# ScalarE copies two kinds of small results out of their PSUM banks, and VectorE works on the copies

## The chip, the core and the metric

The kernel runs on one core of one Trainium2 chip. The metric is device time in microseconds (us), the median of several runs of the whole program. The engines are named as in the profile: PE is TensorE (matrix products), DVE is VectorE, ACT is ScalarE, POOL is GpSimd, SP is the engine whose queue issues nearly all DMAs. A "bank" is a PSUM bank, into which PE writes its results and from which DVE and ACT read them.

## The reference

Two blocks follow one another. The first is attention in which a query sees only the keys that were assigned to the same cluster (4 batches, 8 heads, 768 positions, head width 64, 16 clusters per head). The second is a feed-forward net over the 3072 positions (512 wide, 2048 hidden) with a squared ReLU.

```python
q_assign = argmax(einsum('bhsd,hcd->bhsc', q_n, c_n))   # q, k, centroids normalised
k_assign = argmax(einsum('bhsd,hcd->bhsc', k_n, c_n))
scores = where(q_assign[:, :, :, None] == k_assign[:, :, None, :], q @ k.T / sqrt(D), -1e9)
attn = exp(scores - max);  attn = attn / (sum(attn) + 1e-9)
x = (attn @ v) with heads side by side                  # (3072, 512)
out = (maximum(x @ w_in, 0) ** 2) @ w_out
```

## The kernel before, in words

**Units.** Heads are taken in pairs, so a batch has four pairs (HP = 4) and there are 16 in all. The 768 queries of a pair are taken in two halves h of 384 (TB = 384), and the 768 keys in chunks of 128 (c), two chunks to a unit. Batch 0 goes first through the first halves of all four pairs, then through their second halves; from batch 1 on, a pair's two halves follow each other. Below, (1, 1) means pair 1, second half. All of the change lies in the second halves of batch 0, with one part of it in the preparation for pair 4, the first pair of batch 1.

**A unit's work.** `scores` (L447) has PE form the scores of two chunks in two score banks (records "sc"), ACT takes their exponential (L474), and in batch 0 the mask is already inside the product, so the result is the tile `ex`. From batch 1 on DVE multiplies by the mask (L478). `times_v` (L505) multiplies by v into a bank "av". In all but batch 0's first halves POOL adds the `ex` tiles up over the chunks (L488, L490) into `acc`.

**The end of a half.** `add_up` (L531) has PE multiply `acc` by ones into a bank "sm" of 128x192, and DVE takes the reciprocal, `r` (L545). Two DMAs carry `r` to DRAM (L548) and to a table for a later test (L552), two more bring it back spread over 64 partitions each as `rb` (L551). `finish` (L561) multiplies av by rb into xT (L564, DVE). The tile `r` has one buffer, `rb` has two.

**Preparation of a pair.** For pair 4 and later, the words of q and k are split by ACT (L282), written to DRAM (L283) and read back turned (L293). `logits` (L301) multiplies by the centroids into a bank "lg", and ACT copies it (L312). `number` (L318) turns the logits with three PE transposes into a bank "lt" (L322); DVE takes the maximum over the clusters (L345), compares (L346), weights by an order (L349), takes the maximum again (L352) and casts (L364). `spread` (L401) sends the cluster numbers through DRAM to all partitions.

**Fill work.** Between the attention's products PE is given products of the feed-forward net of batch 0 (`ffn`, L573): "ph" (L578), evacuated by ACT (L585, L586) into gT, and later "po" (L591). While batch 0 runs, the weights are also rounded, 32 pieces in all, each with two ACT instructions (L150, L152), three DVE instructions (L155, L159, L163) and one POOL instruction (L167); their loads (L139) may run four pieces ahead.

**The banks.** These banks come from one ring of two:

```python
ps_f = ctx.enter_context(tc.tile_pool(name="ps_f", bufs=2, space=PSUM))
def bank(name, shape):
    return ps_f.tile(shape, F32, name=name, tag="f")
```

Every "ph", "po", "lg", "lt", "pt", "pb" and, in the halves that the change touches, "sm" takes the next bank of this ring, and has to wait until the tile two places earlier has been read. The scheduler orders each engine's instructions ahead of time; each engine then works its own stream in that order.

## Time and profile before

| | |
|---|---|
| median of 7 runs | 977.77 us (975.77 to 978.62) |
| the profiled execution | 978.39 us, of it 976.6 us span |
| PE busy | 957.2 us, 98% of the span |
| DVE, POOL, ACT busy | 564.4, 380.7, 315.6 us |

The stretches around the change, busy us of each engine:

| stretch (us) | length | PE | DVE | ACT | POOL | granted clock |
|---|---|---|---|---|---|---|
| 80 to 100 | 20 | 18.14 | 19.50 | 15.42 | 17.44 | 1.00 |
| 100 to 120 | 20 | 19.84 | 12.32 | 12.37 | 15.25 | 0.91 |
| 120 to 140 | 20 | 18.13 | 14.71 | 11.33 | 12.22 | 1.00 |
| 140 to 165 | 25 | 23.53 | 16.13 | 12.93 | 15.33 | 1.00 |
| 165 to 190 | 25 | 24.86 | 15.95 | 12.22 | 14.47 | 1.00 |

Read it so: a product of 384 columns has two records, so the "ph" of one f, four products, has eight. A line of the timeline gives start, length, engine, line, operation, operands, number of instructions, and in brackets how long the engine stood idle before them and what ended that. Line numbers in the text and the profile lines are those of the kernel before.

### The profile page before, as it was taken

The page shows a single profiled execution, that of the slowest core. Times are in us where ns is not written, and L with a number is a line of the kernel's source. Part 1 is how long each engine was busy: PE and PEld are TensorE (multiplying, and loading weights), DVE is VectorE, ACT ScalarE, POOL GpSimd, SP SyncE. Part 2 cuts the span into 40 slices and gives each one's busy share as a digit, 9 for nine tenths or more (in the row PEclk, how much of TensorE's full clock was granted, in tenths as well). Part 3 has the DMA queues.
Part 4 walks back from the last instruction along what each step waited for, and adds up shares of the span by engine and source line. Part 5 has one row for each costly group of instructions (what it writes and reads, how often), then busy time and mean ns, then how long its engine had stood idle before and what let it go on. Part 6 is the DMA issues. An engine that isn't in the chain of part 4 may idle for free.

```text
span 976.6 us, 12064 instructions
## 1 busy us (share of the span) xinstructions
PE 957.2 (98%) x4479; PEld 551.6 (56%) x4479; DVE 564.4 (58%) x913; ACT 315.6 (32%) x511; POOL 380.7 (39%) x277
## 2 busy tenths in 40 slices
PE   8999999999999999999999999999999999999997
PEld 4544444443444444444443556888556888556886
DVE  5779666666566665666657966531556431656331
ACT  5887645443444555544322111000111000111000
POOL 1338756555656556565567331002231002331000
PEclk9999999999999999999999999999999999999999
DMA  9667672444545354452310000000000000000000
GB/s 245 197 204 210 182 191 68 118 109 116 133 108 147 105 130 116 108 134 74 77 44 9 19 1 0 22 22 22 1 0 1 22 22 21 1 1 0 22 22 25
DMA packets 127746, 74.54 MB, mean 76 GB/s; under 512 B 90944, under 2 KB 119104, under 8 KB 127680
## 3 DMA queue, kind: packets, MB, share of 16 engines
q1 hardware_dynamic: 125968, 73.26, 28.3%
q8 instruction: 38, 0.62, 0.3%
q10 hardware_dynamic: 1712, 0.43, 0.2%
q14 instruction: 28, 0.23, 0.1%
HBM read 48.27 MB, written 15.86 MB: 66 GB/s over the span
## 4 chain that ended last, share of the span: by engine, by line
PE 89%; DVE 3%; ACT 3%; DMA 2%; issue 1%; SPq 1%; POOL 0%; ACTq 0%; DVEq 0%; POOLq 0%
PE bank L701 22%; PE bank L670 22%; PE po L591 8%; PE ph L578 7%; PE sc L91 7%; PE sc L94 6%; PE av L91 6%; PE av L94 5%; PE sm L91 1%; ACT ex L474 1%; PE lg L91 1%; PE sm L94 1%; DVE ex L478 1%; DVE w_raw L155 1%; DMA rb<-far_r 1%
## 5 line engine op out<-in xcount | busy, mean ns | idle before, releaser
L490 POOL TENSOR_TENSOR acc<-acc,ex 128x768 f32<-128x768 f32 x112 | 207.1, 1849 | 108.5 <-DVE ex L478 93.7
L478 DVE SCALAR_TENSOR_TENSOR ex<-qid,ids,sc 128x384 f32<-128x384 bf16 x288 | 157.8, 608 | 65.7 <-ACT sc L474 41.7
L474 ACT ACTIVATE sc<-sc 128x768 f32<-128x768 f32 x144 | 108.4, 793 | 160.3 <-PE sc L94 142.5
L94 PE MATMUL sc<-qkT 64*128 64x384 f32 x576 | 152.0, 503 | 0.6
L94 PE MATMUL av<-ex,v_raw 128*64 128x384 f32 x576 | 135.5, 491 | 0.0
L659 POOL TENSOR_TENSOR w_s<-w_in 128x256 f32<-128x256 f32 x24 | 18.1, 754 | 274.0 <-PE bank L701 162.0
L640 DVE TENSOR_TENSOR g<-bank,g 128x384 f32<-128x384 f32 x144 | 77.8, 555 | 79.1 <-PE bank L670 77.9
L578 PE MATMUL ph<-xT,w_in 128*128 128x384 f32 x256 | 93.0, 505 | 3.9 <-DVE r L545 2.0
L701 PE MATMUL bank<-w_out,g 128*128 128x256 f32 x432 | 95.2, 379 | 0.0
L591 PE MATMUL po<-w_out,gT 128*128 128x512 f32 x192 | 91.7, 609 | 0.0
L91 PE MATMUL sc<-qkT 64*128 64x384 f32 x192 | 87.2, 534 | 2.7 <-DVE ex L478 2.7
L701 PEld LDWEIGHTS bank<-w_out,g 128*128 128x128 f32 x432 | 82.1, 190 | 11.8
L640 DVE TENSOR_TENSOR osb<-bank,osb 128x256 f32<-128x256 f32 x54 | 22.1, 423 | 107.6 <-PE bank L701 102.2
L94 PEld LDWEIGHTS sc<-qkT 64*128 64x128 f32 x576 | 65.2, 186 | 27.3 <-issue 4.9
L91 PE MATMUL av<-ex,v_raw 128*64 128x384 f32 x192 | 80.4, 500 | 0.0
L488 POOL TENSOR_TENSOR acc<-ex 128x768 f32<-128x768 f32 x28 | 51.7, 1847 | 51.3 <-DVE ex L478 37.9
L578 PEld LDWEIGHTS ph<-xT,w_in 128*128 128x128 f32 x256 | 46.5, 192 | 43.5 <-issue 15.5
L670 PE MATMUL bank<-xT,w_in 128*128 128x384 f32 x192 | 69.8, 487 | 0.0
L670 PE MATMUL bank<-x_t,w_s 128*128 128x384 f32 x192 | 69.7, 486 | 0.0
L670 PE MATMUL bank<-xT,w_s 128*128 128x384 f32 x192 | 69.7, 486 | 0.0
L94 PEld LDWEIGHTS av<-ex,v_raw 128*64 128x64 f32 x576 | 49.5, 137 | 34.2 <-issue 34.0
L701 PE MATMUL bank<-w_t,g 128*128 128x256 f32 x288 | 65.1, 379 | 0.0
(127 smaller groups left out, 1220.2 us busy)
## 6 DMA issues: line engine op xcount, KB each, us to landing
words<-flat SPq DMA_DIRECT2D x24, 384.0 KB
w_raw<-in_moe_w_in_dram SPq DMA_DIRECT2D x16, 512.0 KB
w_raw<-in_moe_w_out_dram SPq DMA_DIRECT2D x16, 512.0 KB
v_raw<-in_v_dram SPq DMA_DIRECT2D x20, 384.0 KB
rb<-far_r SPq DMA_DIRECT2D x64, 96.0 KB
q_raw<-in_q_dram SPq DMA_DIRECT2D x31, 192.0 KB
k_raw<-in_k_dram SPq DMA_DIRECT2D x31, 192.0 KB
out_dram<-osb SPq DMA_DIRECT2D x23, 256.0 KB
```

The source lines that it names most:

```text
L91: last = nc.tensor.matmul(**next(products))
L94: last = nc.tensor.matmul(**product)
L474: last_exp[0] = nc.scalar.activation(out=t[:, 2 * i : 2 * i + 2] if pair < HP else src, in_=src, func=ACT.Exp, scale=SCALE).ins
L478: last_mask[0] = nc.vector.scalar_tensor_tensor(out=t[:, 2 * i + e], in0=qid[pair][1][:, h, e], scalar=ids[pair][:, ch % NB, 2 + ch // NB, ...
L488: nc.gpsimd.tensor_tensor(out=acc[pair, h], in0=t[:, 0:2], in1=t[:, 2:4], op=ALU.add)
L490: nc.gpsimd.tensor_tensor(out=acc[pair, h], in0=acc[pair, h], in1=t[:, 2 * i : 2 * i + 2], op=ALU.add)
L578: nc.tensor.matmul(ph, lhsT=w_in[:, kk, f * P : (f + 1) * P], rhs=xT[b, h][:, kk], start=(kk == 0), stop=(kk == KT - 1),)
L591: nc.tensor.matmul(po, lhsT=gT[f][:, i * P : (i + 1) * P], rhs=w_out[:, f], start=(f == 0), stop=(f == FT - 1),)
L640: nc.vector.tensor_tensor(out=out, in0=bank, in1=to, op=ALU.add)
L659: nc.gpsimd.tensor_tensor(out=s1, in0=a[1][0], in1=a[1][1], op=ALU.add)
L670: nc.tensor.matmul(bank, lhsT=operands[j][0][:, kk], rhs=operands[j][1][:, kk], start=(kk == 0), stop=(kk == H2 - 1),)
L701: nc.tensor.matmul(bank, lhsT=operands[j][0][:, f], rhs=operands[j][1][:, f], start=(f == 0), stop=(f == F2 - 1),)
```

## The change

Two copies by ACT are added. In `add_up`, for batch 0's second halves, ACT copies the sums from their bank into the tile `r`, and DVE takes the reciprocal there in place. In `number`, for pair 4 alone, ACT copies the turned logits from "lt" into a tile of the pool that holds `rb` (two buffers, now shared under one tag), and L345 and L346 read the copy.

```diff
@@ number
         for i in range(NB):
             nc.tensor.transpose(out=lt[:, i], in_=src[:, i * P : (i + 1) * P], identity=ident)
+        if pair == HP:
+            copy = rbp.tile([P, NB, P], F32, name="lt_copy", tag="rb")
+            nc.scalar.copy(out=copy, in_=lt)
+            lt = copy
@@ add_up
         r = once.tile([P, TB // 2], F32, name="r")
+        if pair < HP and h:
+            nc.scalar.copy(out=r, in_=sm)
+            sm = r
         nc.vector.reciprocal(out=r, in_=sm)
...
-        rb = rbp.tile([P, TB], F32, name="rb")
+        rb = rbp.tile([P, TB], F32, name="rb", tag="rb")
```

## The prediction

> **What bounds the kernel now.** I read three views in this order: busy time by engine, PE's waits between 80 and 190 us (where the changed lines run), and the timeline around them. Busy time first:

> ```profile
> PE 957.2 (98%) x4479; PEld 551.6 (56%) x4479; DVE 564.4 (58%) x913; ACT 315.6 (32%) x511; POOL 380.7 (39%) x277
> ```

> PE is the bound: 976.6 - 957.2 leaves it 19.4 us of idle time in the whole span. Nothing that merely unloads DVE can pay; only PE's idle time and a lowered clock are to be had. PE's waits on others in the stretch (total, times, longest):

> ```profile
> PE ph L578 <- DVE r L545: 2.0, 1, 2.0
> PE ph L578 <- DVE best L346: 1.9, 1, 1.9
> PE sc L91 <- DVE ex L478: 1.5, 1, 1.5
> ```

> The first two are fill products that want a bank which DVE has still to read: the sums of (0, 1), and the turned logits of pair 4. Those are the two tiles that the change copies. The timeline shows why DVE is late and what ScalarE does meanwhile:

> ```profile
> 94.95 1.51 ACT L474 ACTIVATE ex<-sc 128x768 f32<-128x768 f32 x2 [1.87 <-PE sc L94]
> 95.14 0.34 PE L94 MATMUL sm<-acc,ups 128*32 128x192 f32 x3
> ...
> 96.35 0.68 ACT L150 ACTIVATE w_out<-w_raw 128x512 f32<-128x512 f32 x1
> 96.91 1.92 DVE L163 TENSOR_SCALAR w_out<-w_raw 128x512 uint32<-128x512 uint32 x1
> ...
> 98.76 1.34 DVE L545 RECIPROCAL r<-sm 128x192 f32<-128x192 f32 x1
> ...
> 100.16 8.41 PE L578 MATMUL ph<-xT,w_in 128*128 128x384 f32 x20 [2.02 <-DVE r L545]
> ```

> The sums are in their bank at 95.48 (95.14 + 0.34). DVE, busy 19.50 of the 20 us from 80 to 100, is rounding weights and takes the reciprocal only from 98.76 to 100.10. PE has nothing left at 98.14 and stands 2.02 us. Then it runs slowly: 20 records in 8.41 us are 0.42 each, where another fill line has 14 in 4.71, 0.336 each. The granted clock in windows of 1 us (length, PE busy, clock, DMA share, GB/s) says why:

> ```profile
> 101.00:102.00 1.00, 1.00 (x4) 0.72 1.28 291
> 102.00:103.00 1.00, 1.00 (x3) 0.50 1.27 290
> 103.00:104.00 1.00, 1.00 (x3) 0.50 1.00 239
> 104.00:105.00 1.00, 1.00 (x3) 0.57 0.98 308
> ```

> It loses 0.28 + 0.50 + 0.50 + 0.43 = 1.71 us, the only such loss that I find after the start. I take it for a consequence of the stall, since it follows 1 us behind it.

> The second place:

> ```profile
> 121.11 0.49 PE L322 MATMUL lt<-ident,lgs 128*128 128x128 f32 x3
> 121.50 0.53 ACT L586 ACTIVATE gT<-gT 128x384 f32<-128x384 f32 x1
> 122.93 0.49 ACT L585 ACTIVATE gT<-ph 128x384 f32<-128x384 f32 x1 [0.89 <-PE ph L578]
> 123.07 1.92 DVE L163 TENSOR_SCALAR w_out<-w_raw 128x512 uint32<-128x512 uint32 x1
> 124.92 0.55 DVE L345 TENSOR_REDUCE mx<-lt 128x24 f32<-128x384 f32 x1
> 125.50 0.56 DVE L346 TENSOR_TENSOR best<-lt,mx 128x384 bf16<-128x384 f32 x1
> 126.20 0.88 PE L578 MATMUL ph<-xT,w_in 128*128 128x384 f32 x2 [1.87 <-DVE best L346]
> ```

> The logits lie turned at 121.60; DVE is done with them at 126.06. PE's granted clock is 1.00 throughout here.

> **The change part by part.** I also read the changed kernel's instruction order, engine by engine. Outside the second halves of batch 0 it is the same; POOL's order is the same throughout.

> *The copy of the sums, (0, 1).* It stands on ScalarE right after the exponentials that end at 96.35 and ahead of L150. Its price is not in the trace. The nearest rows are ScalarE copies out of a bank: 128x384 in 482 ns (L312), 128x256 in 372 ns (L644), 12x128 in 250 ns (L408). The slope of the first two, 110 ns for 128 columns, gives 372 - 55 = 0.32 us for 192; the ends are 0.25 and 0.37. The bank is free at 96.35 + 0.32 = 96.67, which is 1.5 us before PE wants it at 98.14. The stall of 2.02 goes, and with it, as I read it, the 1.71 of clock.

> What is late next: PE then does the first f in eight records to 98.14 + 8 x 0.336 = 100.83, the next to 103.5, and half of a third, which needs ScalarE's L585 of the first. ScalarE, whose work behind the copy (L150, L152, L585, L586, two exponentials, two more roundings) ended at 102.21, ends it at 102.53 and L585 at 103.02: 0.5 us in time. Those ScalarE instructions are what queues behind the copy; its 2.24 us of idle before 104.45 takes up the 0.32.

> *The copy of the logits, pair 4.* On ScalarE it comes after L586, so at 122.03 by the old clock, and with 0.48 us (L312, same shape) ends at 122.51. It fits into the 0.89 us for which ScalarE waited. PE wants the bank at 122.82, when its preceding fill product ends. It stands 0.3 us inside, so all of the 1.87 goes. (In the new order one fill product also moves ahead of the av products; the same work in another order, at nothing.)

> *The other three sums.* PE does not wait for L545 there: at (1, 1) and (2, 1) fill work lies between, at (3, 1) the scores from 169.22 to 170.78 cover the reciprocal that ends at 170.72. These copies gain nothing. They cost ScalarE 3 x 0.32, at moments when it goes on to wait for PE (0.59 us at 135.55, 0.71 at 148.08, 1.83 at 170.24): nothing. At (1, 1) and (2, 1) they stand behind two exponentials, so the reciprocal comes 1.2 us later against PE than now; then come far_r, rb and L564, for which DVE waited 2.0 and 1.85 us on DMA already, and whose bank PE wants only 13 us on (L564 at 140.99, next av at 154.31).

> *Waits added and moved.* The copy, not the reciprocal, now waits for the DMAs that read the former `r` (L548, L552). These are issued 20 us or more ahead of (0, 1), (1, 1) and (3, 1), and 8 us ahead of (2, 1) (136.22 against 144.73). `rb` shares its two buffers with the logits' copy: the copy's buffer was last read at about 81 us; the rb of (1, 1) now waits for L564 of (0, 1), 20 us earlier. On SP one weight load (L139) moves ahead of the rb of (0, 1). It waits for POOL's L167 (104.75 + 1.67), while rb waited for far_r until 106.98, so the issue moves 0.4 us; but 512 KB at the 200 to 300 GB/s of this stretch are some 2 us ahead of it, so I put L564 of (0, 1) at 113 to 114 instead of 111.2. In exchange five DVE rounding steps go ahead of it and use the 5.94 us that DVE stood there. The bank which L564 frees is wanted at 127 now, at about 121 after. A load of v also goes behind one of k; it has 20 us.

> *VectorE on the copies.* Neither L545 (1357 ns) nor L345 and L346 (557, 548 ns) is on the path afterwards. Bounds: no change, or a stretch such as L349, which reads SBUF alone, shows (349 to 1293 ns): 0.7 us on an engine that is idle 5 to 9 us in each of the next stretches. I take nothing. [...]

> *Sum.* 2.02 + 1.71 + 1.87 = 5.60 us. From 126 us on PE is busy all but some 5 us, and other engines are led by it, so I expect it to reach the end. 978.39 (the profiled execution) - 5.60 = 972.8 us. That execution lies 0.6 above the median of 977.77, from which it would be 972.2.

> [...] The trace has the clock at half 1 us after a gap of 2.02. [...]

> **Rivals.**

> 1. *The clock loss does not go with the stall,* or comes back elsewhere: the 1.87 us stall had none, so 2.02 may just be enough in some executions and not in others. 978.39 - 3.89 = 974.5. For it: the 2.85 us spread of the seven runs.
> 2. *The logits' copy comes too late.* It has 0.3 us; behind a slow L282 or L586 PE would still wait, as now at most 1.87: 978.39 - 3.73 = 974.7.
> 3. *Given back at batch 1's first masks.* PE's third wait (1.47 us before 164.13) is for L478, which follows the last rounding steps on DVE. If DVE does not come forward, that wait grows by what was gained: 978.4. Against it: DVE stood 3.40 us just before, at 156.99, waiting for ScalarE's L152, which itself follows PE's scores.
> 4. *Slower: ScalarE held by the sums.* A copy waits for the sum products, which wait for POOL's last addition, and exponentials stand behind it. At (0, 1) POOL ended at 92.79 (88.55 + 4.24), 2.15 us ahead of the products. If POOL falls back by more than that, ScalarE stands, nothing is gained, and the copies (4 x 0.32 + 0.48 = 1.76) lie on the path: 980.2. Against it: POOL's order is unchanged, and at (1, 1) it is 20 us ahead.

> **How the numbers follow.** Forecast 0.60, rivals 1 and 2 together 0.25, rival 3 0.10, rival 4 0.05. About 0.2%, or 2 us, is what a measurement of this kernel can tell from no change. Faster: 0.60 + 0.25 = 0.85; same 0.10; slower 0.05. The range takes in the forecast and rivals 1 and 2: up to 974.7 and some 0.9 more for run-to-run spread, 975.6; down to the 972.2 counted from the median, less 1.6 (the 1.47 us wait before 164.13, should DVE come forward more than PE), 970.6.

> **What would show it.** Right: no wait of "ph" for r, and none for best; copies of about 0.32 and 0.48 us ending before PE asks; clock 1.00 from 100 to 105; the lg products of pair 4 some 3.7 us earlier (109.4 instead of 113.1) and the first scores of batch 1 some 5.6 earlier (151.4 instead of 157.0); the end earlier by as much. Wrong: "ph" waits for an ACT copy in place of DVE; the wait for L478 near 158 us grows beyond 1.5; a stretch at half clock elsewhere.

## The result, and the profile after

The changed kernel takes 973.42 us (median of 16 runs, 972.45 to 975.19) beside 977.65 for the kernel before (42 runs, 974.79 to 980.98). The ratio is 0.9959, with a 95% interval of 0.9949 to 0.9968: 4.0 us less, by the interval 3.1 to 5.0. Measured again in another group of runs it was 0.9948 (0.9932 to 0.9963). The forecast was 972.8, so the sign, the places and most of the size came out. The sum of 5.60 us is more than the runs give.

The profiled execution took 973.86 us, span 972.0. The changed lines moved down in the file: L345, L346, L478, L545, L564, L578 and L585 are L350, L351, L483, L554, L573, L587 and L594 after; the new copies are L326 (logits) and L552 (sums). Busy time, page of the kernel after:

```profile
PE 956.2 (98%) x4479; PEld 551.2 (57%) x4479; DVE 568.2 (58%) x913; ACT 316.9 (33%) x516; POOL 381.6 (39%) x277
```

ACT has five instructions more and 1.3 us more. PE's waits from 80 to 190 us, kernel after (total, times, longest):

```profile
PE sc L91 <- DVE ex L483: 1.4, 1, 1.4
PE ph L587 <- DVE xT L573: 0.5, 1, 0.5
PE ph L587 <- ACT gT L594: 0.2, 1, 0.2
```

The two waits of "ph" for r and for best are gone. The wait for the mask is as it was (1.45 us against 1.47). The 0.5 lies ahead of the change, before 84 us; a second execution of the kernel before has it too (0.48). The 0.2 is new. The timeline, kernel after, first place:

```profile
97.01 0.33 ACT L552 COPY r<-sm 128x192 f32<-128x192 f32 x1
98.73 5.43 PE L587 MATMUL ph<-xT,w_in 128*128 128x384 f32 x16
98.87 1.34 DVE L554 RECIPROCAL r<-r 128x192 f32<-128x192 f32 x1
102.67 0.68 ACT L150 ACTIVATE w_out<-w_raw 128x512 f32<-128x512 f32 x1 [0.72 <-DMA w_raw<-in_moe_w_out_dram]
103.81 0.47 ACT L594 ACTIVATE gT<-ph 128x384 f32<-128x384 f32 x1
104.33 1.56 PE L587 MATMUL ph<-xT,w_in 128*128 128x384 f32 x4 [0.17 <-ACT gT L594]
```

DVE is as late with the reciprocal as it was (98.87 against 98.76), but PE no longer asks for it: the bank is free at 97.34 and PE starts "ph" at 98.73 without a wait. Its 16 records take 0.339 us each, and the clock is 1.00 in every window of 1 us from 100 to 105. The new 0.17 us comes from a load of weights: L150 waits 0.72 us for it, and gT stands behind L150 in ACT's queue. The second place, kernel after:

```profile
118.75 2.10 PE L587 MATMUL ph<-xT,w_in 128*128 128x384 f32 x6
118.80 0.55 ACT L595 ACTIVATE gT<-gT 128x384 f32<-128x384 f32 x1
118.94 3.96 POOL L495 TENSOR_TENSOR acc<-acc,ex 128x768 f32<-128x768 f32 x2
119.22 0.49 ACT L326 COPY lt_copy<-lt 128x384 f32<-128x384 f32 x1
121.14 0.54 DVE L350 TENSOR_REDUCE mx<-lt_copy 128x24 f32<-128x384 f32 x1
121.72 1.60 DVE L351 TENSOR_TENSOR best<-lt_copy,mx 128x384 bf16<-128x384 f32 x1
```

ACT frees the bank at 119.71, where DVE would have done so only at 123.32. PE does not stand here: its line at 118.75 has no wait, and its six records run on until 120.85.

Start times of PE's products show where the time went. The first number is before, the second after:

| product | before | after | difference |
|---|---|---|---|
| sums of (0, 1) | 95.0 | 95.6 | +0.6 |
| lg of pair 4 | 113.05 | 110.36 | -2.69 |
| sums of (1, 1) | 130.3 | 125.3 | -5.0 |
| first scores of batch 1 | 157.04 | 152.10 | -4.94 |
| last sums | 531.3 | 526.8 | -4.5 |
| span | 976.6 | 972.0 | -4.6 |

The execution after came 0.66 us late to the stretch (the first scores at 93 us), for reasons ahead of the change. From there to batch 1's first scores it gained 0.66 + 4.94 = 5.60 us, which is the forecast sum, and to the end of the span 0.66 + 4.6 = 5.3 us. So for these two executions the sum is about right (that it agrees to the hundredth is chance, since the new wait of 0.17 us is in it too); for the kernels as a whole it is too large, and the experiments look for the reason.

### The profile page after: what moved, and what is told of

It is laid out like the page before. It is cut to its first block, busy times and chain, and to the rows that moved or that the text cites. A ratio compares the mean times of both kernels' runs of the same rounds, so it can differ in the third digit from the quotient of the medians.

```text
span 972.0 us, 12075 instructions
## 1 busy us (share of the span) xinstructions
PE 956.2 (98%) x4479; PEld 551.2 (57%) x4479; DVE 568.2 (58%) x913; ACT 316.9 (33%) x516; POOL 381.6 (39%) x277
## 4 chain that ended last, share of the span: by engine, by line
PE 82%; issue 5%; POOL 4%; DMA 4%; DVE 2%; SPq 2%; ACT 0%; ACTq 0%; POOLq 0%; DVEq 0%
PE bank L710 22%; PE bank L679 22%; PE po L600 8%; PE ph L587 7%; PE sc L91 6%; PE sc L94 5%; PE av L91 5%; PE av L94 5%; POOL w_in L167 2%; POOL acc L495 1%; PE sm L91 1%; DMA rb<-far_r 1%; DVE ex L483 1%; PE lg L91 1%; DMA qid<-far 1%
## 5 line engine op out<-in xcount | busy, mean ns | idle before, releaser
L483 DVE SCALAR_TENSOR_TENSOR ex<-qid,ids,sc 128x384 f32<-128x384 bf16 x288 | 157.8, 608 | 63.9 <-ACT sc L479 45.4
L94 PE MATMUL sc<-qkT 64*128 64x384 f32 x576 | 152.4, 503 | 0.7
L94 PE MATMUL av<-ex,v_raw 128*64 128x384 f32 x576 | 135.4, 491 | 0.0
L587 PE MATMUL ph<-xT,w_in 128*128 128x384 f32 x256 | 91.6, 498 | 0.7 <-DVE xT L573 0.5
L91 PE MATMUL sc<-qkT 64*128 64x384 f32 x192 | 87.2, 534 | 2.6 <-DVE ex L483 2.5
L94 PEld LDWEIGHTS sc<-qkT 64*128 64x128 f32 x576 | 65.0, 186 | 27.9 <-issue 5.8
L91 PE MATMUL av<-ex,v_raw 128*64 128x384 f32 x192 | 80.3, 500 | 0.0
L94 PEld LDWEIGHTS av<-ex,v_raw 128*64 128x64 f32 x576 | 49.6, 137 | 34.1 <-issue 34.0
L587 PEld LDWEIGHTS ph<-xT,w_in 128*128 128x128 f32 x256 | 45.7, 189 | 39.5 <-issue 11.2
L710 PE MATMUL bank<-w_t,g_s 128*128 128x256 f32 x288 | 65.1, 379 | 0.0
```

Source lines behind the costliest of these rows:

```text
L91: last = nc.tensor.matmul(**next(products))
L94: last = nc.tensor.matmul(**product)
L483: last_mask[0] = nc.vector.scalar_tensor_tensor(out=t[:, 2 * i + e], in0=qid[pair][1][:, h, e], scalar=ids[pair][:, ch % NB, 2 + ch // NB, ...
L587: nc.tensor.matmul(ph, lhsT=w_in[:, kk, f * P : (f + 1) * P], rhs=xT[b, h][:, kk], start=(kk == 0), stop=(kk == KT - 1),)
L710: nc.tensor.matmul(bank, lhsT=operands[j][0][:, f], rhs=operands[j][1][:, f], start=(f == 0), stop=(f == F2 - 1),)
```

## The experiments

Theory A: the gain is the two removed waits and the clock loss behind the first one, and the execution that was profiled before happened to be a dear one. Rival B: one copy does the work and the other only moves the wait. Rival C: the clock loss is not tied to the stall. The first four kernels ran on one chip together, beside 35 runs of the kernel before (977.69).

**1. The kernel before, once more.**

> The kernel before, unchanged, for its own spread. Theory (half clock follows the 2.02 us stall of the fill products at the sums of (0, 1), but only in a part of the executions, by where the stall falls): the 2.0 and 1.9 us stalls recur in the profile, the span of single runs falls into groups about 1.7 us apart, with the mean granted clock lower (0.998 against 1.0) in the slower group. Rival (the clock loss has nothing to do with the stall): the stretch at half clock, if it recurs, lies somewhere else in the profile, and no such groups show. Time against before: same, 0.0 +- 1 us for both.

Measured: 977.42 us (975.11 to 980.38), ratio 1.0003 (0.9990 to 1.0016). PE's waits from 80 to 190 us in this second profile of the kernel before:

```profile
PE sc L91 <- DVE ex L478: 1.8, 2, 1.4
PE ph L578 <- DVE r L545: 1.5, 1, 1.5
PE ph L578 <- DVE best L346: 1.1, 1, 1.1
PE ph L578 <- DVE xT L564: 0.5, 1, 0.5
```

The same program has the same stalls, but of 1.45 and 1.12 us instead of 2.02 and 1.87, and the clock is not lowered between its start and its end. The expected groups of runs 1.7 us apart do not show in the twelve times. The size of a term was a matter of the execution.

**2. The copy of the sums of (0, 1) alone.**

```diff
-        if pair < HP and h:
+        if pair == 0 and h:
             nc.scalar.copy(out=r, in_=sm)
             sm = r
```

The copy in `number` is left out.

> Only the copy of the sums of (0, 1); the other three sums and the turned logits are read by VectorE in their banks. Theory (each stall is a wait for one bank, and they add up): the stall for r is gone, the stall for best of about 1.9 us stays; 2.0 us faster in every run, and 3.7 against runs with the half-clock stretch: 2.0 to 3.7 us faster than before, the half clock near 101 us gone. Rival A (the gain is that VectorE's and SP's orders change, all parts together): about none. Rival B (the clock loss is not the stall's): 2.0 us and a stretch at half clock still there.

Measured: 975.31 us, ratio 0.9977 (0.9965 to 0.9989), 2.2 us less. PE's waits, this kernel:

```profile
PE sc L91 <- DVE ex L483: 1.5, 1, 1.5
PE ph L587 <- DVE best L351: 1.3, 1, 1.3
PE ph L587 <- ACT gT L594: 0.3, 1, 0.3
```

The first stall goes, the second stays, and the small wait for gT appears here too. No half clock is left near 101 us, but this profile has one from 161.6 us on, behind the wait for the mask.

**3. The copy of the logits alone.** The copy in `add_up` is left out.

> Only the copy of pair 4's turned logits. Theory: the stall for best of 1.9 us is gone, the stall of 2.0 us for r and the half clock behind it stay: 1.9 us faster than before (1.4 to 2.4). Rival A (parts only work together): 0. Rival B (the logits' gain was only that the first stall had gone): below 0.5 us.

Measured: 975.75 us, ratio 0.9982 (0.9972 to 0.9993), 1.8 us less. The wait for best is gone, that for r is 2.13 us, and no half clock follows it.

**4. The copies of the last three sums alone.** `if 0 < pair < HP and h:`, no copy in `number`.

> Only the copies of the sums of (1, 1), (2, 1) and (3, 1). Theory: TensorE waits for none of these banks; both stalls stay; 0.0 us (-0.5 to +0.5). Rival (three copies of 0.33 us on ScalarE lie on the path): 1.0 us slower. Rival (unloading the banks earlier helps everywhere): 1 us or more faster.

Measured: 977.71 us, ratio 1.0004 (0.9991 to 1.0018): nothing. Both stalls stay (1.91 and 1.26 us). A half clock follows neither of them; one follows the wait for the mask, from 164.3 us on.

The parts add up: 2.2 + 1.8 + 0 = 4.0 us, as measured for all, though by its interval each part is known only to about 1 us. Rival B falls.

**5. No copy; VectorE's backlog taken away instead.** The main loop counts `rounding` up by 4 at each step u and takes up one piece of weight rounding for each 3. Here one piece that stood just ahead of the reciprocal of (0, 1) is taken up three steps later. Experiments 5 to 8 ran together on another chip, where the kernel before took 978.46 (20 runs).

```diff
-        rounding += 4
+        rounding += 4 - 3 * (u == 15) + 3 * (u == 18)
```

> The kernel before, without any copy: one piece of weight rounding (on VectorE 0.68 + 1.41 + 1.92 us in the profile of before) that stands just ahead of the reciprocal of (0,1) is taken up three steps later. TensorE's order is the same. Theory (the stall at the reciprocal is VectorE's backlog alone, and the copy buys only that the bank no longer waits for it): the reciprocal starts as soon as the sums are there, the stall of 1.5 to 2.0 us goes, about 975.5 us, as with the copies of (0,1) alone (975.3); the stall at the mask's first product stays, 1.1 to 1.9. Rival (the reciprocal's own 1.34 us in the bank is what TensorE waits for, so a copy of 0.33 is needed): a stall of about 1 us is left and the time is near 976.7. Second rival (the moved piece comes back at a later wait): about 977.6.

Measured: 980.32 us, ratio 1.0021 (1.0010 to 1.0033), slower. The second rival came true, and at a dearer place. ("The mask's first product" in the expectation is the "ph" that waits for best; its stall stays, 1.02 us here.) Timeline of this kernel, reciprocal, PE, then ACT and PE at 118 us:

```profile
95.57 1.36 DVE L545 RECIPROCAL r<-sm 128x192 f32<-128x192 f32 x1 [0.72 <-PE sm L94]
98.09 6.72 PE L578 MATMUL ph<-xT,w_in 128*128 128x384 f32 x20
...
117.89 0.67 ACT L150 ACTIVATE w_out<-w_raw 128x512 f32<-128x512 f32 x1 [1.64 <-DMA w_raw<-in_moe_w_out_dram]
119.74 0.51 ACT L585 ACTIVATE gT<-ph 128x384 f32<-128x384 f32 x1
120.31 0.55 PE L322 MATMUL lt<-ident,lgs 128*128 128x128 f32 x3 [2.21 <-ACT gT L585]
```

The reciprocal starts 3.2 us earlier and PE does not wait for it. So the first stall was VectorE's backlog, not the reciprocal's own 1.36 us. But ACT's rounding step L150 now comes before its load has landed, gT stands behind it in order, and PE waits 2.21 us for gT. Windows of 1 us behind that (length, PE busy, clock, DMA share, GB/s):

```profile
121.00:122.00 1.00, 1.00 (x4) 0.77 0.84 143
122.00:123.00 1.00, 1.00 (x3) 0.50 0.48 180
123.00:124.00 1.00, 1.00 (x6) 0.50 0.78 311
124.00:125.00 1.00, 1.00 (x6) 0.52 0.70 156
```

0.23 + 0.50 + 0.50 + 0.48 = 1.71 us are lost here, as much as behind the 2.02 us stall before. The same execution loses 1.70 more from 165.9 on, behind the wait for the mask. That is more than the median's 2.1 us, so a part of this profile is its own.

**6. No copy; one piece more ahead of the reciprocal.**

```diff
-        rounding += 4
+        rounding += 4 + 2 * (u == 15) - 2 * (u == 17)
```

> The kernel before, without any copy, the other way: one more piece of rounding (0.72 + 1.94 + 1.91 us on VectorE) is taken up ahead of the reciprocal of (0,1). TensorE's order is the same. Theory (a microsecond of this stall is a microsecond of the end): the stall grows from 1.5 to 2.0 us to some 6, the time to about 982 us. If the half clock follows the gap by its length, nearly all executions show a mean granted clock of 0.997 or less, and 1.7 us more: about 983.7. If it follows by chance, the clocks are as mixed as those of before (0.995 to 1.000). Rival (the stall is partly hidden, since ScalarE's and GpSimd's work behind it goes on): under 980.

Measured: 982.03 us, ratio 1.0040 (1.0026 to 1.0055), 3.9 us slower. PE's line at the first stall in this kernel's waits:

```profile
PE ph L578 <- DVE r L545: 4.6, 1, 4.6
```

The stall is 2.6 to 3.1 us longer than in the two executions of before, and a stretch at half clock begins as it ends (102.4 to 105.8, 1.71 us lost). All six runs have a mean granted clock of 0.997 or less. Of the 72 runs of the kernel before that stand beside the three groups of experiments 26 have that, and of the 12 in experiment 1 none. (The mean clock is a rough sign. Each profile also has a piece at half clock in its last 0.2 to 3.5 us, when PE's work is done. With a long such piece 0.998 occurs without a stretch behind a stall, as in the profile of the kernel after; with a short one it occurs with a stretch, as in the profile of the kernel before. So 0.998 is not counted, and the count can miss a stretch.) 4.59 less the first stall's mean of 1.88 (worked out below) is 2.7 us, and 1.71 in all runs instead of about a third of them is 1.1 more: 3.8 of the 3.9. So a longer stall is paid in full, and this one, as far as the mean clocks tell, brings the half clock with it each time. The expected 983.7 was for a stall of 6 us.

**7. The logits copied three times.** In the kernel after, `for _ in range(3): nc.scalar.copy(out=copy, in_=lt)`.

> The kernel after, with the turned logits copied three times by ScalarE, so that their bank comes free 2 x 0.48 = 0.96 us later. The slack behind the copy is some 0.3 us in the profile of after. Theory (TensorE now depends on ScalarE alone there): a new wait of TensorE for ScalarE's copy of 0.5 to 0.7 us, 974.0 us, still nothing for VectorE. Rival (other banks of that pool are free by then): no wait, 973.4.

Measured: 975.26 us, ratio 0.9964 (0.9950 to 0.9977). This is inconclusive for the slack. The scheduler put a group of av products ahead of the "ph" that needs the bank, so that PE asks at 121.51, and the copies end at 120.67: no wait there. The wait of 0.72 us in this execution is at 104.26, the one for gT behind a late load again.

**8. The kernel after, with the last two pieces of rounding earlier.**

```diff
-        rounding += 4
+        rounding += 4 + 3 * (u in (21, 22))
```

> The kernel after, with the last two pieces of weight rounding taken up earlier, so that VectorE has only masks left at batch 1's second pair of scores. Theory: the last stall in this stretch (TensorE for the mask of L483, 1.45 us at 159.2) goes or shrinks to under 0.5, about 972.0 to 972.5 us, and with it one more place where the clock can be halved. Rival (masks alone keep VectorE busy there; the wait is theirs): 1.4 us stays, 973.4. Second rival (the pieces taken up earlier make a new wait at the last sums): 973.4 or more.

Measured: 971.19 us (970.94 to 972.89), ratio 0.9931 (0.9916 to 0.9946), the best kernel of the study. Its interval lies under that of the first measurement of the kernel after, and overlaps that of the second. PE's only wait from 80 to 190 us:

```profile
PE ph L587 <- DVE xT L573: 0.9, 1, 0.9
```

The wait for the mask at 159 is gone. Ahead of these masks DVE now stands idle, where it had rounding to do before; timeline of this kernel:

```profile
153.98 2.19 DVE L483 SCALAR_TENSOR_TENSOR ex<-qid,ids,sc 128x384 f32<-128x384 bf16 x4 [1.84 <-POOL w_out L167]
```

**9. The same shift in the kernel before, without copies.**

> The kernel before, without any copy, with the last two pieces of weight rounding taken up earlier (the edit of both_round_ahead alone). both_round_ahead stood 0.0069 of the time (6.7 us) under before, the changed kernel 4.1. Theory (each stall is its own term and the parts add up): the stall at the second pair of batch 1's masks goes, the other two stay: 2.6 us under before, ratio 0.997 to 0.998. Rival (the pieces can only go earlier since the copies made room on VectorE): a new or longer stall at the sums, ratio 0.999 or more.

Measured: 976.45 us, ratio 0.9984 (0.9973 to 0.9996), 1.6 us less. The rival has its part: the wait for the mask goes, but one of the other sums gets a wait of its own. Timeline of this kernel, DVE and PE at the sums of (2, 1):

```profile
147.24 0.68 DVE L155 SCALAR_TENSOR_TENSOR w_raw<-w_raw 128x512 uint32<-128x512 uint32 x1
...
149.70 1.41 DVE L163 TENSOR_SCALAR w_out<-w_raw 128x512 uint32<-128x512 uint32 x1
151.02 1.34 DVE L545 RECIPROCAL r<-sm 128x192 f32<-128x192 f32 x1
152.42 4.78 PE L578 MATMUL ph<-xT,w_in 128*128 128x384 f32 x14 [1.90 <-DVE r L545]
```

The sums are there at 147.7, six rounding instructions stand ahead of the reciprocal, and PE waits 1.90 us. In experiment 8 ACT's copy covers this very place. So the copies that gain nothing in experiment 4 are worth something once VectorE's work is moved.

**10. The kernel after, once more.**

> The changed kernel again, beside the run above: ratio 0.9959 as before, no wait of TensorE for the sums or the mask, one of 1.4 to 1.5 us for the mask of L483. Theory of the clock: in its runs the mean granted clock is 0.998 or more nearly always, in before's 0.997 or less in about a third.

Measured: 973.04 us (972.49 to 974.50), ratio 0.9948 (0.9932 to 0.9963). Up to 165 us its profile has one wait of PE after 80, 1.45 us for the mask; not even gT's 0.17.

## Why the prediction came out as it did

**The two stalls: right in place and cause, the second too large.** PE stood for DVE's reading of two banks, and each copy removes its own stall (experiments 2 and 3). In the four profiles that keep the first one as it was (the two of before, experiments 3 and 4) it was 2.02, 1.45, 2.13 and 1.91 us, mean 1.88; in the four that keep the second (the two of before, experiments 2 and 4) it was 1.87, 1.12, 1.28 and 1.26, mean 1.38. The forecast took 2.02 and 1.87 from one execution, and for the second that execution was the highest of the four: 0.5 us too much.

**The clock: the step that failed in size is "I take it for a consequence of the stall" with its full 1.71 us.** It is a consequence, but not of every stall. Where a half clock appears between the start and the last 3.5 us in any profile here, it begins 1.1 to 1.4 us behind a stall, or, after the 4.59, as it ends. After the first 22 us the twelve profiles have 30 stalls of PE from 1.44 to 2.75 us, 12 of them the wait of 1.6 us for POOL at the last sums. Five were followed by it (2.02, 1.46, 1.45, 2.21, 1.45) and 25 were not (among them 1.87, 1.91, 2.13 and 2.75). Of the 17 from 0.5 to 1.3 us, between 80 and 300 us, none was. The last section shows what sorts the long ones. Each time the half clock cost 1.70 or 1.71 us. Rival 1 was thus half right: the price is paid in a part of the executions. Runs of the kernel before at a mean clock of 0.997 or less were 12 of 35, and took 2.2 us longer than the others (978.92 against 976.73 on average); 12/35 x 2.2 is 0.75 us (with the 12 runs of experiment 1, 0.56). None of the 24 runs of the kernel after has a mean clock of 0.997 or less. The mean clock does not tell behind which stall a run lost it, so 0.75 is no measurement of the first stall's share alone.

**What that leaves.** 1.88 + 1.38 + 0.75 is 4.0 us, less the new wait for gT, 0.25 in the mean of those five. That is within 3.1 to 5.0. This sum mixes means of four profiles with means of runs, so it is an account that fits, not a proof of each tenth. The 3.89 (2.02 + 1.87) that rival 1 of the prediction counts with lies close to the measured 4.0, but by chance: it takes the two stalls 0.63 us too large and leaves out the 0.75.

**What is late next: slightly wrong.** I had ACT's L594 0.5 us in time. It was late by 0.17, 0.35 and 0.72 us in three profiles (after, experiments 2 and 7), and in time in two (8 and 10). My sum of ACT's instructions left out that L150 waits for its load, 0.72 us in the profile after, and 0.89, 1.27 and 0.61 us in those of experiments 2, 7 and 10. The stall had not simply covered this: in the two profiles of before the same L150 ran at 100.97 and 101.68 us without a wait, so the load had landed by then; in these four it came only at 101.9 to 102.7. Why it did is open. (The fill row that I read as 14 records in 4.71 us is 14 in 4.78 in the profile, 0.341 each; that moves the end of the first f by 0.04 us and changes nothing.)

**The copies: right.** 0.33 and 0.49 us against 0.32 and 0.48; the bank free at 97.34, forecast 96.67, which is the same after the 0.66 of late arrival. lg of pair 4 came at 110.36 (forecast 109.4, again with 0.66), batch 1's first scores at 152.10 (forecast 151.4).

**The other three sums: right for this kernel** (experiment 4), with the reserve that experiment 9 adds. None of the rivals 2 to 4 came: no wait at the logits' bank, and the wait for L478 not longer (1.45). ACT stood 0.95 us for the sums of (3, 1), before 164.40, but it then had to wait 0.56 us for PE's next scores as well, and PE did not wait for it.

**The rb of (0, 1): the direction right, the size too large.** L564 of (0, 1), L573 after, came at 112.71, with the 0.66 taken off 0.85 later than before; I had put 2 to 3.

**VectorE on the copies: no effect on the end.** The reciprocal takes 1.34 us from SBUF as from the bank. The compare takes 1.60 us where it took 0.56, and the traces show what it goes with. The compare on the copy ends at 123.32, 0.42 us after POOL's addition ends at 122.90, and in all five profiles with this copy the two ends are 0.41 to 0.42 us apart. L349 (L354 after), which has two SBUF inputs in every kernel, takes 0.56 us where no POOL instruction runs as it starts; in all 128 cases after the first 20 us of the twelve profiles in which one had 0.14 us or more to run, L349 ended 0.41 to 0.42 us after it. L346 out of the bank takes 0.55 to 0.56 us in all of its 175 runs in the same stretch, 124 of them with POOL busy throughout. So the copy puts the compare behind POOL, here by 1.04 us, and it costs nothing because no one waits for it.

## What to carry to other kernels

Where the busiest engine waits for a bank, ask which engine frees it and what stands in that engine's queue: a cheap copy by an engine that is in time (here 0.33 and 0.49 us on ACT) frees the bank without making the late engine faster (DVE's reciprocal starts at 98.87 beside 98.76). Behind the removed stall look for what is late next, here a load that lands just in time or too late (L150 waited 0.61 to 1.27 us for it in four profiles), and then take up the next stall: with the bank safe, fill work could be moved on VectorE for another gain (ratio 0.9931 in experiment 8, beside 0.9959 and 0.9948 without the move). Size a term by several executions: a stall read from one profile may be half as long again as the next one's (here 2.02 beside 1.45 us, 1.87 beside 1.12), and a clock loss behind it (here 1.71 us) may be there in one execution and missing in the next. Before moving an input of VectorE into SBUF, look at what GpSimd does at that time: here the compare took 1.60 us beside 0.56, and ended 0.42 us after GpSimd's addition.

## What the runs showed of the hardware

The half clock comes in pieces of one size. Each stretch behind a stall lost 1.70 or 1.71 us, so it lasted 3.4. Two executions (experiments 3 and 9) have one of 13.7 us near the start, from 8 to 22 us, four times as long, and are the slowest runs of their kernels (978.73 and 981.51). In experiment 5 the two stretches begin at 121.54 and 165.92, 44.38 us apart, 13.0 times the 3.413 us between the fall and the rise in the profile of before. The length of a stall alone does not say whether a half clock follows: behind stalls of 1.45 or 1.46 us it came three times, behind the one of 2.75 us it did not.
